# Attention products in one buffer by token blocks, with a new order of the work

## The chip, the cores and the metric

The kernel runs on one core of one Trainium2 chip. A core has five engines that work side by side, each through a queue of its own in the order in which the program issued it: TensorE (PE: matmuls, and PEld: its weight loads), VectorE (DVE), ScalarE (ACT), GpSimd (POOL) and SyncE (SP, which here only issues transfers). The metric is the time of the whole kernel on the device in microseconds. The time before is 206.82 us, the median of three runs (206.54 to 207.95).

## What is computed

The input x has 2048 tokens of 640 values. After a layer norm two branches are computed from the same normalized tokens and added to x: an attention over a sliding window, and a two-layer network.

```python
xn = layernorm(x)                                   # 2048 x 640
# A: 32 heads of 20; each token looks at 8 tokens, 2 apart, itself and back
q, k, v = split(xn @ wqkv)
logits = sum_d q[s] * k[s - 2*w], w = 0..7          # masked where s - 2*w < 0
o = sum_w softmax(logits * 20**-0.5) * v[s - 2*w]
A = o @ wo
# B: 640 -> 1536 -> 640
B = gelu(xn @ w1 + b1) @ w2 + b2
out = x + A + B
```

## The kernel before

The tokens are cut into four chunks of 512 (`NCH`, `CH`), a chunk into four blocks of 128 (`BPC`, `P`). Everything but the first normalization and the last output works on transposed data: 640 values are five tiles (`KT`) of 128 partitions, and the tokens lie along the row. The columns of the query, key and value weights are taken with a stride of 5, so that the 20 values of a head lie on 4 neighbouring partitions in all five tiles.

For each chunk:
- The rows of x are normalized (`do_xn`) and transposed: by TensorE for chunk 0 (`do_tp`, `do_tc`), by a transposing DMA of SP for the others (`do_td`, L291).
- Projections: `do_pj` (L334; for chunk 0 in smaller pieces at L347 and L378), five matmuls of 512 columns each into one of four accumulator banks, taken out to bf16 by ScalarE (`do_pc`, L398).
- Logits: VectorE multiplies the queries by the keys shifted by each window offset (`do_qk`, L431). The products lie in two buffers, `half[0]` for offsets 0 to 3 and `half[1]` for 4 to 7, each [offset, tile, 512 tokens]. The sum over the 20 values of a head is made partly by VectorE (`do_pa`, L463: tiles 0+1 and 2+3; and in chunks 2 and 3 also `do_pb`, L468: everything into tile 0) and the rest by matmuls with a 0/1 matrix (`do_lg`, L477: 24 matmuls in chunks 0 and 1, 8 in chunks 2 and 3). These write all eight offsets into one PSUM tile `L`.
- Softmax over the eight offsets (`do_cp` to `do_attn`, L513 to L554): copies, maximum, difference, exponential, sum, reciprocal by a logarithm and an exponential, product. Its small maxima and sums use `half[0]` as scratch in chunk 0.
- Expansion: a DMA of SP (`expand`, L573) writes each head's weights onto its four partitions, block by block, into `ax` for chunks 0 and 2 and into spent rows of `x_sb` for 1 and 3.
- Values: VectorE multiplies the shifted values by these weights (`do_av`, L588, one block and one half of the offsets at a time, 32 in all), adds the eight offsets up in three steps over the whole chunk (`do_add`, L597) and a last one into `oT` (`do_ot`, L602).
- The network: `do_f1` (L609) and the gelu (`do_ge`, L625) into 18 turning buffers.
- Output of chunks 0 to 2: `do_t` (L691) adds, for each fifth of the output columns, twelve products of the network in four pieces (`t..0` to `t..3`) and then five of the attention (`t..4`); ScalarE adds the bias (`do_u`, L694), SP turns it back by a transposing DMA (`do_ut`, L698), and POOL adds it by an accumulating DMA onto x in the output (`do_ud`, L703), which SP had copied there (`do_xp`, L300).
- Output of chunk 3: `do_o` (L647) with tokens on the partitions, VectorE adds x (`do_dc`, L659), and four stores follow (`do_dd`, L664). For this chunk the second bias is added to x by VectorE (`do_xl`, L304), from a copy `b2bc` of the bias in all partitions (L159).

The order of the work is written out by hand: `ORDER` (L39) names 628 pieces, and the kernel issues them one after the other; nothing is moved afterwards. A name is a function, a chunk and a part: `qk201` is `do_qk` of chunk 2, block pair 0, half 1. Each engine works through those of its own in that order, and waits where a piece needs something of another engine. GpSimd is not among the engines that are held to the order (L818).

Of the kernel before, what the change touches and what calls it, by code (L numbers as in the profile page):

```python
# [17 lines left out]
P = 128  # L18
# [15 lines left out]
LEVEL = (1, 1, 3, 3)  # L34
ACT_STATS = (2, 3)
# [4 lines left out]
pad01 pad02 st00a st00 sum1 rs00 mean1 neg1 sq1 xn00a xn00b tp00a wa tp00b wb tc00a tc00b rs01 ga xn01a xn01b gb2  # L40
tp01a gb3 tp01b tc01a tc01b gb4 gd gc0 ge st03a st02a tb hj100 st03 rs03 st02 xn03 b1 rs02 xn02 st11a st13a st10a st13
st12a st10 st12 st11 gc4 gc1 tp03 tc03 tp02 tc02 ho hj101 hc101 hj102 hc102 hj011 hc100 hc011 rs1 hj112 hc112 rc1 xn12
tc12 qk000 hj012 qk001 hj201 xn10 tc10 hc012 hc201 hj211 hc211 hj110 hc110 hj010 hc010 f10_1 pk pa000 xn13 hj111 tc13
xn11 tc11 ldx ld2 pa010 hc111 qk010 hj212 qk011 pa001 pa011 hc212 f10_5 f10_11 ge0_11 ge0_1 hj200 ge0_5 hc200 hj202
pj103 pc103 pj104 pc104 pad11 pj110 pc110 pj102 pc102 pj112 hc202 lg0 pc112 su20 cp0b cp0a m0b mask pj111 mx0b ex0b
m0a pj114 pc114 ss0b mx0a pj101 pc101 ri0b pj113 pc113 ex0a pc111 pj100 at0b pc100 ss0a su22 qk111 ri0a qk101 pj124
pc124 at0a qk110 pa111 qk100 pa110 pa101 f11_3 pa100 f11_10 ge1_3 ldo f10_8 ge0_8 hj210 hc210 xp0 su21 f10_2 ge0_2
su23 ge1_10 f10_0 ng2 ge0_0 f10_7 f10_3 f10_4 sq22 ge0_3 ge0_7 f11_5 sq21 ge0_4 sq23 f10_6 ge0_6 pj121 xs0 sq20 rs2
t040 t041 f11_0 rc2 pj122 pc122 xn22 pc121 xd0 xp1 xp2 tc22 xn23 tc23 lg1 cp1a f10_10 f11_1 ge1_1 ge1_0 xn21 av020
cp1b ge0_10 t000 t001 t042 t002 xn20 f10_9 av030 av000 f11_9 ge1_9 av001 av011 tc21 f11_11 ge0_9 tc20 ge1_5 m1 av021  # L50
mx1 ex1 av031 pj120 pc120 t003 pj123 pc123 t043 pad12 av010 pj221 pc221 ss1 pj224 ri1 ad01 at1 pc224 pj220 pj200 su33
pc220 ad00 ad02 ot0 pc200 pj214 pc214 xs1 su32 av131 pj202 pc202 pj213 pc213 pad21 pj212 pc212 su31 pj204 pj210 pc210
pc204 av121 pj211 pj203 pj201 su30 ng3 sq32 sq30 t004 u00 t044 u04 sq31 pc211 xd1 av101 av100 av111 av120 av130 sq33
ut00 t010 ud00 t011 t012 t013 t014 pc201 av110 u01 rs3 rc3 pj222 pc203 pad22 ad10 t030 t031 f11_6 xn32 tc32 t032 ad11
ad12 t020 t021 t022 xn30 tc30 f11_2 pc222 ge1_2 t023 t033 t034 xn33 tc33 t024 ge1_6 ot1 f11_4 qk201 qk200 qk210 xn31
ge1_4 qk211 pa200 pa211 pa201 u03 pa210 pb202 pb212 pb204 pj223 f12_1 pc223 f11_8 ge1_8 f12_6 ut01 ge2_6 ge2_1 pb214
t130 tc31 pj310 pc310 pj303 pc303 pj301 pc301 ge1_11 f11_7 pj311 pc311 pj302 pj312 pc302 pj313 pc312 ge1_7 pc313 u02
ut02 pj300 f13_3 f12_10 pc300 pj322 pc322 pj320 pc320 pj304 ge2_10 ut03 ut04 ud01 pad31 pc304 pj314 pc314 ud02 ge3_3
f13_9 f12_7 ge3_9 ge2_7 lg2 cp2b qk310 cp2a m2 mx2 f13_5 ge3_5 qk311 f13_2 pj324 pc324 pj321 ex2 ss2 pa311 t131 t132
t133 ri2 at2 xd2 t140 t134 ud03 pc321 u13 ge3_2 f13_7 t141 t142 t143 f13_4 f13_0 t100 ge3_7 t101 f12_11 ge2_11 pj323  # L60
t102 t103 qk300 f13_6 t104 ge3_6 f13_10 ge3_10 ge3_0 t144 u14 f12_0 ge3_4 pc323 ge2_0 qk301 xs2 pa300 pa310 pa301
pb312 pb302 pb314 f13_1 pb304 lg3 xl0 cp3a cp3b av230 ge3_1 av201 m3 av210 pad32 t110 f12_3 f12_2 t111 t112 mx3 t113
t114 u10 ut10 ex3 f12_8 f12_9 o300 av200 ss3 u11 ut11 av220 ri3 at3 av231 t120 av211 av221 o301 ud10 t121 t122 ge2_3
t123 f13_8 ge2_2 ge3_8 ge2_9 ad21 ad20 t124 xd3 xs3 ad22 u12 ut12 ot2 av321 av331 f12_5 f13_11 ge3_11 f12_4 ge2_5 t230
o310 ge2_4 av320 t231 ge2_8 t232 o320 av330 av311 av300 av310 av301 ad30 t200 ud11 t233 t201 t202 t203 o321 ud04 t204
ut13 ut14 u20 ut20 t234 ad31 u23 t210 t211 t212 t213 ud12 t214 t220 u21 t221 o322 t222 t223 t224 u22 o311 o330 o312
ud13 o313 ud20 o302 t240 ut21 t241 t242 t243 o323 t244 o331 o303 o332 o333 ad32 ot3 o324 xl1 o314 o304 dl2 ud14 dh2
dl1 u24 o334 dh1 dl0 ohi ud21 ut22 ud22 ut23 ut24 dd2 dd1 dh0 dd0 dl3 dh3 dhi dlo ud23 ud24
# [4 lines left out]
def kernel(  # L73
# [46 lines left out]
    b2bc = consts.tile([P, D], BF16, name="b2bc")  # L120
    wqkv_v = A_wqkv.rearrange("(t p) n -> p t n", p=P)
    b2_bcast = bass.AP(tensor=B_b2.tensor, offset=B_b2.offset, ap=[[0, P], [1, D]])
# [23 lines left out]
    def do_ldx():  # L146
        for n in range(2, NCH):
            load_x(n * BPC, (n + 1) * BPC)
# [7 lines left out]
    def do_ldo():  # L156
        for a, b in COLS:
            nc.sync.dma_start(wo2[:, a:b], A_wo.rearrange("(p t) n -> p t n", t=KT)[:, a:b])
        nc.sync.dma_start(b2bc[:], b2_bcast)  # L159
# [142 lines left out]
    def do_xl(pair):  # L302
        rows_ = x_sb[:, (NCH - 1) * BPC + 2 * pair : (NCH - 1) * BPC + 2 * pair + 2, :]
        nc.vector.tensor_tensor(  # L304
            out=rows_, in0=rows_, in1=b2bc[:].unsqueeze(1).to_broadcast([P, 2, D]), op=ALU.add
        )
# [106 lines left out]
    half = [prodp.tile([P, W // 2, KT, CH], BF16, name=f"half{i}") for i in range(2)]  # L413

    def window(src, h, cs):

        first = PAD - DIL * (W // 2 * h) + cs.start
        row = src[:, :, first : first + cs.stop - cs.start]
        (part, n_part), (tile_step, n_tile), (_, n_col) = row.ap
        return bass.AP(  # L420
            tensor=row.tensor,
            offset=row.offset,
            ap=[[part, n_part], [-DIL, W // 2], [tile_step, n_tile], [1, n_col]],
        )

    def do_qk(n, pair, h):
        cs = slice(pair * 2 * P, (pair + 1) * 2 * P)
        q, k, at = qkv_tile(n, 0), qkv_tile(n, 1), cs
        if n == 0:
            q, k, at = pair_of(0, pair), pair_of(1, pair), slice(0, 2 * P)  # L430
        nc.vector.tensor_tensor(  # L431
            out=half[h][:, :, :, cs],
            in0=q[:, :, at].unsqueeze(1).to_broadcast([P, W // 2, KT, 2 * P]),
            in1=window(k, h, at),
            op=ALU.mult,
        )
# [22 lines left out]
    def do_pa(n, h, c):  # L459

        cs = slice(c * 2 * P, (c + 1) * 2 * P)
        even, odd = (half[h][:, :, i : KT - 1 : 2, cs] for i in range(2))
        nc.vector.tensor_tensor(out=even, in0=even, in1=odd, op=ALU.add)  # L463

    def do_pb(n, h, t):

        first = half[h][:, :, 0, :]
        nc.vector.tensor_tensor(out=first, in0=first, in1=half[h][:, :, t, :], op=ALU.add)  # L468

    def do_lg(n):  # L470
        L = psL.tile([P, W, P], F32, tag="L", name="L")
        tiles["L", n] = L
        ts = (range(KT), (0, 2, 4), (0, 4), (0,))[LEVEL[n]]
        for h in range(2):
            for t in ts:
                for j in range(BPC):
# [3 lines left out]
                        rhs=half[h][:, :, t, j * P : (j + 1) * P],  # L480
# [13 lines left out]
    scratch = half[0][:].rearrange("p w t c -> p (w t c)")  # L494
# [4 lines left out]
    def room(n, i, dtype, off):  # L499

        size = W // 2 * P // PARTS[n] * (2 if dtype == F32 else 1)
        if PARTS[n] == 1:
            flat = attn_tile(n)[:].rearrange("p w c -> p (w c)")[:, 0:size]
        else:
            flat = scratch[:, off + i * size : off + (i + 1) * size]
# [72 lines left out]
    def do_xd(n):  # L578
        expand(nc.sync, n, (0, 1))

    def do_xs(n):
        expand(nc.sync, n, (2, 3))


    def do_av(n, j, h):
        cs = slice(j * P, (j + 1) * P)
        ws = slice(W // 2 * h, W // 2 * (h + 1))
        nc.vector.tensor_tensor(  # L588
            out=half[h][:, :, :, cs],
            in0=window(qkv_tile(n, 2), h, cs),  # L590
            in1=ax_view(n)[:, j, ws, :].unsqueeze(2).to_broadcast([P, W // 2, KT, P]),
            op=ALU.mult,
        )

    def do_add(n, k):
        a, b = ((half[0][:, 0:2], half[1][:, 0:2]), (half[0][:, 2:4], half[1][:, 2:4]), (half[0][:, 0:2], half[0][:, 2:4]))[k]
        nc.vector.tensor_tensor(out=a, in0=a, in1=b, op=ALU.add)  # L597

    def do_ot(n):
        oT = otp.tile([P, KT, CH], BF16, tag="oT", name="oT")  # L600
        tiles["oT", n] = oT
        nc.vector.tensor_tensor(out=oT[:], in0=half[0][:, 0], in1=half[0][:, 1], op=ALU.add)  # L602
# [52 lines left out]
    def do_dc(bl, hi):  # L655

        b, cs = (NCH - 1) * BPC + bl, slice(CH, D) if hi else slice(0, CH)
        room = half[1][:].rearrange("p w t c -> p (w t c)")[:, bl * D : (bl + 1) * D]
        nc.vector.tensor_tensor(out=room[:, cs], in0=out_ps(bl, hi), in1=x_sb[:, b, cs], op=ALU.add)  # L659

    def do_dd(bl, cs, eng):
        b = (NCH - 1) * BPC + bl
        room = half[1][:].rearrange("p w t c -> p (w t c)")[:, bl * D : (bl + 1) * D]
# [52 lines left out]
    for name in "tb b1 mean1 ho ldx ld2 ldo ohi mask pk".split():  # L716
# [33 lines left out]
    for n in range(NCH):  # L750
# [22 lines left out]
        for h in range(2):  # L773
            for pair in range(2):
                piece(f"qk{n}{pair}{h}", do_qk, n, pair, h)
            for j in range(BPC):
# [79 lines left out]
```

## Time and profile before

| | |
|---|---|
| median of the runs | 206.82 us |
| the profiled execution's own time | 206.68 us |
| its span, first to last instruction | 204.9 us |
| granted TensorE clock | 1.0 |
| PE / DVE / ACT / POOL busy | 98% / 91% / 62% / 10% |
| DVE, L431 and L588 (products) | 44.5 us in 16, 45.7 us in 32 |
| DVE, L463 and L468 (halvings) | 18.8 us in 16, 9.3 us in 8 |
| DVE, L597 and L602 (sums over the window) | 33.6 us in 12, 6.0 us in 4 |
| DVE, L304 (bias) | 1.6 us in 2 |
| transfers | 22.91 MB, mean 112 GB/s |

Busy is the time in which an engine has an instruction at work. Instructions overlap at their ends, so that the mean of one is longer than its pitch, the time from one start to the next in a row without waits. A row of the profile names the line, the engine, the operation, what it writes and reads, its shape (partitions x elements), how many there are, the busy time and the mean in nanoseconds, then the idle time of the engine just before them and what ended it. The span does not hold all of an execution's time: 1.8 us lie around it.

### The profile page before, as it was taken

How to read it: one execution, taken by the hardware profiler on the slowest of the kernel's cores; microseconds unless marked ns; L12 is line 12 of the kernel's file. 1: busy time of each engine (PE TensorE's matmuls, PEld its weight loads, DVE VectorE, ACT ScalarE, POOL GpSimd, SP SyncE). 2: the span in 40 equal slices, each digit the busy share in tenths (PEclk: the TensorE clock that was granted, in tenths of full speed). 3: DMA queues.
4: the chain of work that ended last, by engine and by line, in shares of the span. 5: the costliest groups of instructions: out<-in, count | busy, mean ns of one | idle time of the engine just before them, and what ended most of it. 6: DMA issues, size and time to landing. Idle time of an engine off the chain costs nothing.

```text
span 204.9 us, 2932 instructions
## 1 busy us (share of the span) xinstructions
PE 200.6 (98%) x1132; PEld 105.6 (52%) x1132; DVE 187.3 (91%) x177; ACT 128.0 (62%) x235; POOL 20.9 (10%) x33
## 2 busy tenths in 40 slices
PE   7999999999999999999999999999999999999994
PEld 2898754554444555444445554444444444445452
DVE  2899995799899999999999997999989999999963
ACT  5689967999899887858755576571785650211100
POOL 2000000000000000020010070000002207022520
PEclk9999999999999999999999999999999999999999
DMA  6997599507932027132430193044014699656635
GB/s 204 386 397 201 73 358 392 207 0 151 292 85 64 3 32 172 26 26 67 91 26 0 30 98 29 0 76 129 0 29 51 91 192 80 51 52 76 48 46 141
DMA packets 36400, 22.91 MB, mean 112 GB/s; under 512 B 24994, under 2 KB 34082, under 8 KB 36386
## 3 DMA queue, kind: packets, MB, share of 16 engines
q1 hardware_dynamic: 28144, 20.55, 36.8%
q0 software_dynamic: 7920, 1.97, 13.6%
q8 instruction: 9, 0.15, 0.3%
q10 hardware_dynamic: 322, 0.20, 0.3%
q14 instruction: 5, 0.04, 0.1%
HBM read 10.00 MB, written 4.59 MB: 71 GB/s over the span
## 4 chain that ended last, share of the span: by engine, by line
PE 96%; DMA 2%; SPq 0%; DVE 0%; issue 0%
PE T L691 27%; PE hps L609 25%; PE pps L334 24%; PE gps L378 7%; PE lo L647 5%; DMA wq_sb<-in_A_wqkv_dram 2%; PE both L647 2%; PE L L477 2%; PE gps L347 1%; PE hi L647 1%; PE tp L279 0%; SPq L126 0%; DVE half L659 0%; PE tb L454 0%
## 5 line engine op out<-in xcount | busy, mean ns | idle before, releaser
L609 PE MATMUL hps<-xnT,w_sb 128*128 128x512 bf16 x240 | 55.9, 379 | 0.0
L431 DVE TENSOR_TENSOR half<-qT,kT 128x5120 bf16<-128x5120 bf16 x16 | 44.5, 2821 | 1.4 <-PE L L477 1.4
L691 PE MATMUL T<-hT,w_sb 128*128 128x512 bf16 x180 | 42.8, 379 | 0.0
L609 PEld LDWEIGHTS <-w_sb 128*128 128x128 bf16 x240 | 23.3, 98 | 27.9 <-issue 0.8
L703 POOL DMA_DIRECT2D out_dram<-x_sb x15 | 19.5, 1406 | 176.8 <-DMA x_sb<-x_sb 176.7
L691 PEld LDWEIGHTS <-w_sb 128*128 128x128 bf16 x180 | 17.3, 98 | 20.6 <-issue 0.4
L625 ACT ACTIVATE hT<-hps,bT 128x512 bf16<-128x512 f32 x36 | 23.7, 693 | 6.2 <-PE hps L609 6.1
L694 ACT ACTIVATE x_sb<-T,bT 128x512 bf16<-128x512 f32 x15 | 10.3, 689 | 23.4 <-PE T L691 23.4
L588 DVE TENSOR_TENSOR half<-vT,ax 128x2560 bf16<-128x2560 bf16 x16 | 23.1, 1485 | 1.4 <-PE L L477 1.4
L588 DVE TENSOR_TENSOR half<-vT,x_sb 128x2560 bf16<-128x2560 bf16 x16 | 22.6, 1486 | 0.0
L597 DVE TENSOR_TENSOR half<-half,half 128x5120 bf16<-128x5120 bf16 x8 | 22.3, 2821 | 0.1
L463 DVE TENSOR_TENSOR half<-half 128x2048 bf16<-128x2048 bf16 x16 | 18.8, 1221 | 0.0
L691 PE MATMUL T<-oT,wo 128*128 128x512 bf16 x75 | 18.1, 379 | 0.0
L334 PE MATMUL pps<-xnT,wq_sb 128*128 128x512 bf16 x75 | 18.1, 379 | 0.0
L334 PE MATMUL pps<-xnT,wk_sb 128*128 128x512 bf16 x75 | 18.0, 379 | 0.0
L334 PE MATMUL pps<-xnT,wv_sb 128*128 128x512 bf16 x75 | 18.0, 379 | 0.0
L172 ACT ACT_TABLE_LOAD x12 | 15.4, 1283 | 0.9 <-PEq L840 0.7
L334 PEld LDWEIGHTS <-wv_sb 128*128 128x128 bf16 x75 | 8.8, 117 | 7.6
L334 PEld LDWEIGHTS <-wk_sb 128*128 128x128 bf16 x75 | 8.7, 118 | 7.6 <-issue 0.4
L262 ACT ACTIVATE xn<-x_sb,nmr,rstd 128x640 bf16<-128x640 bf16 x12 | 10.8, 921 | 2.9 <-DVE nmr L252 2.2
L334 PEld LDWEIGHTS <-wq_sb 128*128 128x128 bf16 x75 | 8.8, 117 | 7.2
L398 ACT CAST vT<-pps 128x512 bf16<-128x512 f32 x15 | 8.6, 580 | 5.8 <-PE pps L334 5.8
(95 smaller groups left out, 232.1 us busy)
## 6 DMA issues: line engine op xcount, KB each, us to landing
ax<-attn SPq DMA_DIRECT2D x8, 256.0 KB, 4.3
x_sb<-attn SPq DMA_DIRECT2D x8, 256.0 KB, 4.7
x_sb<-in_A_x_dram SPq DMA_DIRECT2D x3, 640.0 KB, 6.2
w_sb<-in_B_w_dram SPq DMA_DIRECT2D x2, 960.0 KB, 11.3
w_sb<-in_B_w_dram SPq DMA_DIRECT2D x4, 480.0 KB, 8.7
out_dram<-x_sb SPq DMA_DIRECT2D x3, 640.0 KB, 7.3
out_dram<-x_sb POOLq DMA_DIRECT2D x15, 128.0 KB, 4.0
wq_sb<-in_A_wqkv_dram SPq DMA_DIRECT2D x1, 800.0 KB, 5.1
```

The source lines that it names most:

```text
L172: nc.scalar.preload_act_table_set(name)
L334: nc.tensor.matmul(ps[:], lhsT=wqkv_p[which][:, ti, to, :], rhs=xnT[:, ti, :], start=(ti == 0), stop=(ti == KT - 1),)
L378: nc.tensor.matmul(ps[:, to - a, :], lhsT=wqkv_p[which][:, ti, to, :], rhs=tiles["xnT", 0][:, ti, pair * 2 * P : (pair + 1) * 2 * P], star ...
L431: nc.vector.tensor_tensor(out=half[h][:, :, :, cs], in0=q[:, :, at].unsqueeze(1).to_broadcast([P, W // 2, KT, 2 * P]), in1=window(k, h, at ...
L463: nc.vector.tensor_tensor(out=even, in0=even, in1=odd, op=ALU.add)
L588: nc.vector.tensor_tensor(out=half[h][:, :, :, cs], in0=window(qkv_tile(n, 2), h, cs), in1=ax_view(n)[:, j, ws, :].unsqueeze(2).to_broadca ...
L597: nc.vector.tensor_tensor(out=a, in0=a, in1=b, op=ALU.add)
L609: nc.tensor.matmul(ps[:], lhsT=w1_sb[:, ti, ft * P : (ft + 1) * P], rhs=tiles["xnT", n][:, ti, :], start=(ti == 0), stop=(ti == KT - 1),)
L625: nc.scalar.activation(hT, tiles["hps", n, ft][:], ACT.Gelu_apprx_tanh, bias=bT[:, ft : ft + 1], scale=1.0)
L647: nc.tensor.matmul(out_ps(bl, hi), lhsT=lhs, rhs=rhs[:, CH:D] if hi else rhs[:, 0:CH], start=pc == 0 and k == 0, stop=pc == 4 and k == len ...
L691: nc.tensor.matmul(ps[:], lhsT=lhs, rhs=rhs, start=pc == 0 and k == 0, stop=pc == 4 and k == len(srcs) - 1)
L703: nc.gpsimd.dma_start(dst, src, accum_op=ALU.add)
```

## The change

- One buffer `prod` [block, offset, tile, 128 tokens] replaces the two halves, so that all products of a block of 128 tokens lie together. `do_qk` and `do_av` make the products of one block with all eight offsets in one instruction: 16 of 128x5120 each.
- `do_pa` adds tiles 2 and 3 onto tiles 0 and 1 (not odd onto even) for a pair of blocks and all offsets: 8 of 128x4096. `do_pb` adds tile 1, then tile 4, for the chunk: 4 of 128x4096. The logits matmuls are as many as before and read the new places.
- The sum over the window becomes `do_ac` (a block, 128x2560, 16), `do_ad` (a pair of blocks, 128x2560, 8) and `do_ot` (a pair of blocks, 128x1280, 8).
- The second bias of the last chunk is added to x by one accumulating DMA of POOL (`do_xb`) that reads the bias from HBM once for each token; `b2bc`, its load and the two additions of VectorE go.
- The expansions become pieces of one block (`xe`), chunk 0's softmax scratch moves to `ax`, and the x of chunk 2 is loaded in two transfers.
- GpSimd is held to the order too, and `ORDER` is new throughout. The table `BY_DMA` could move sums to POOL; it is empty.

```diff
-    half = [prodp.tile([P, W // 2, KT, CH], BF16, name=f"half{i}") for i in range(2)]
+    prod = prodp.tile([P, BPC, W, KT, P], BF16, name="prod")
-    def do_qk(n, pair, h):
+    def do_qk(n, j):
         nc.vector.tensor_tensor(
-            out=half[h][:, :, :, cs],
-            in0=q[:, :, at].unsqueeze(1).to_broadcast([P, W // 2, KT, 2 * P]),
-            in1=window(k, h, at),
+            out=prod[:, j],
+            in0=q[:, :, at].unsqueeze(1).to_broadcast([P, W, KT, P]),
+            in1=window(k, at),
...
+    def rows_of(a, b):
+        return prod[:, a:b].rearrange("p j w t c -> p (j w) (t c)")
+    def do_pa(pair):
+        rows = rows_of(2 * pair, 2 * pair + 2)
+        low, high = rows[:, :, 0 : 2 * P], rows[:, :, 2 * P : 4 * P]
+        nc.vector.tensor_tensor(out=low, in0=low, in1=high, op=ALU.add)
+    def do_pb(t):
+        rows = rows_of(0, BPC)
+        first = rows[:, :, 0:P]
+        nc.vector.tensor_tensor(out=first, in0=first, in1=rows[:, :, t * P : (t + 1) * P], op=ALU.add)
...
-                        rhs=half[h][:, :, t, j * P : (j + 1) * P],
+                        rhs=prod[:, j, W // 2 * h : W // 2 * (h + 1), t, :],
...
-    def do_av(n, j, h):
+    def do_av(n, j):
-            out=half[h][:, :, :, cs],
+            out=prod[:, j],
...
+    def do_ac(n, j):
+        low, high = (prod[:, j, W // 2 * h : W // 2 * (h + 1)] for h in range(2))
...
+            nc.vector.tensor_tensor(out=low, in0=low, in1=high, op=ALU.add)
+    def do_ad(n, pair):
+        low, high = (prod[:, 2 * pair : 2 * pair + 2, 2 * i : 2 * i + 2].rearrange("p j w t c -> p j (w t c)") for i in range(2))
+        nc.vector.tensor_tensor(out=low, in0=low, in1=high, op=ALU.add)
+    def do_ot(n, pair):
+        oT = get(("oT", n), lambda: otp.tile([P, KT, CH], BF16, tag="oT", name="oT"))
+        a, b = (prod[:, 2 * pair : 2 * pair + 2, w].rearrange("p j t c -> p t j c") for w in range(2))
+        out = oT[:, :, 2 * pair * P : (2 * pair + 2) * P].rearrange("p t (j c) -> p t j c", j=2)
+        nc.vector.tensor_tensor(out=out, in0=a, in1=b, op=ALU.add)
...
-    def do_xl(pair):
-        rows_ = x_sb[:, (NCH - 1) * BPC + 2 * pair : (NCH - 1) * BPC + 2 * pair + 2, :]
-        nc.vector.tensor_tensor(
-            out=rows_, in0=rows_, in1=b2bc[:].unsqueeze(1).to_broadcast([P, 2, D]), op=ALU.add
-        )
+    def do_xb():
+        rows_ = x_sb[:, (NCH - 1) * BPC :, :]
+        b2_all = bass.AP(tensor=B_b2.tensor, offset=B_b2.offset, ap=[[0, P], [0, BPC], [1, D]])
+        nc.gpsimd.dma_start(rows_, b2_all, accum_op=ALU.add)
...
-        for n in range(2, NCH):
-            load_x(n * BPC, (n + 1) * BPC)
+        for n in (4, 5, 6):
+            load_x(n * BPC // 2, (n + 1 + n // 6) * BPC // 2)
...
-    engines = {getattr(mybir.EngineType, e) for e in ("PE", "DVE", "Activation", "SP")}
+    engines = {getattr(mybir.EngineType, e) for e in ("PE", "DVE", "Activation", "SP", "Pool")}
```

Of the order, the places that the prediction speaks of (old, then new):

```
- tp00a wa tp00b wb ... ga xn01a xn01b gb2 tp01a gb3 tp01b tc01a
+ wa ... tp00a ... tp00b ... ga xn01a wb gb2 tp01a xn01b st03a tc01a
- tc12 ... tc10 ... tc13 ... tc11 ldx ld2
+ tc11 ... tc10 ... ldx ... tc13 tc12 ... ld2
- xs0 ... xd0 xp1 xp2 ... tc22 ... tc23 ... tc21 ... tc20
+ tc22 ... tc20 ... xe02 ... xe03 tc23 xe00 ... tc21 ... xe01 ... pj210
- ... ad32 ot3 o324 xl1 o314 o304 ... o334 ... ohi
+ ... ot30 ... o304 ... o314 ... ot31 dl1 ... o324 ... o334 ... ohi
```

More of the change, by code (lines that the diff above doesn't have):

```diff
@@ L34 @@
 LEVEL = (1, 1, 3, 3)
+BY_DMA = ((), (), (), ())
 ACT_STATS = (2, 3)
@@ L45 @@
[L45 to L49, printed above, removed]
@@ L805 @@
         last = BPC - 1
-        for pair in range(2):
-            piece(f"xl{pair}", do_xl, pair)
         for bl in range(BPC):
```

132 lines of the change are left out of this document (58 added, 74 removed).

## The prediction

> **What bounds the kernel now.** I read the page first (busy shares, slices, chain), then the groups by shape, the waits, and the timeline of each engine. The page says that TensorE is the bound from almost the first microsecond to the last:
>
> ```profile
> span 204.9 us, 2932 instructions
> PE 200.6 (98%) x1132; PEld 105.6 (52%) x1132; DVE 187.3 (91%) x177; ACT 128.0 (62%) x235; POOL 20.9 (10%) x33
> PE   7999999999999999999999999999999999999994
> PEclk9999999999999999999999999999999999999999
> PE 96%; DMA 2%; SPq 0%; DVE 0%; issue 0%
> ```
>
> A busy PE need not be PE at its peak, so I checked the pitch: in the chain "1.08 PE hps x5" repeats, that is 0.216 us for each 512-column matmul at a granted clock of 1.0, and from 6.32 us (the first real product, released by the load of wq) to 202.17 us (the last one) piece follows piece with no gap over 0.3 us. Around these 195.85 us lie 6.3 us of head and 2.7 us of tail. The span is 204.9 and the execution's own time 206.68, so 1.78 us lie outside the span; 206.68 is 0.14 below the median of the runs (206.82).
>
> Now VectorE, which the change is about. By shape:
>
> ```profile
> L431 DVE TENSOR_TENSOR half<-qT,kT 128x5120 bf16<-128x5120 bf16 x16 | 44.5, 2821 | 1.4 <-PE L L477 1.4
> L588 DVE TENSOR_TENSOR half<-vT,ax 128x2560 bf16<-128x2560 bf16 x16 | 23.1, 1485 | 1.4 <-PE L L477 1.4
> L597 DVE TENSOR_TENSOR half<-half,half 128x5120 bf16<-128x5120 bf16 x8 | 22.3, 2821 | 0.1
> L463 DVE TENSOR_TENSOR half<-half 128x2048 bf16<-128x2048 bf16 x16 | 18.8, 1221 | 0.0
> ```
>
> And who is late for whom:
>
> ```profile
> DVE half L588 <- PE L L477: 1.4, 2, 0.9
> DVE half L431 <- PE L L477: 1.4, 1, 1.4
> PEld L477 <- DVE x_sb L304: 0.4, 1, 0.4
> PEld L477 <- DVE half L463: 0.4, 1, 0.4
> ```
>
> VectorE waits for TensorE (it cannot overwrite the products until the logits matmuls L477 have read them). The other way round only two weight loads wait, 0.4 us each, and the matmul row shows no gap there. So the two engines run abreast, VectorE just ahead. The change can win on TensorE only what lies in the head and the tail, and can lose as soon as VectorE, or a transfer, comes late.
>
> **VectorE, part by part.** In the timeline four L431 take 11.03 us and eight L588 take 11.30, so one starts (11.03 - 2.82)/3 = 2.74 us and (11.30 - 1.49)/7 = 1.40 us after the one before. Between the two sizes that is 0.522 ns an element and 0.067 us fixed; it gives 1.135 us for 2048 elements, and the four L463 (4.63 us) give 1.14. By this an instruction of 4096 elements costs 2.20 and one of 1280 costs 0.735. Then:
> - Query-key products: 16 of 5120 before and after; no change.
> - Attention-value products: 32 x 1.40 become 16 x 2.74: -1.1.
> - First halvings: 16 x 1.14 become 8 x 2.20: -0.6. Second ones: 8 x 1.14 become 4 x 2.20: -0.3.
> - Sums over the window: 12 x 2.74 + 4 x 1.40 = 38.5 become 16 x 1.40 (one block each) + 8 x 1.40 (pairs) + 8 x 0.735 = 39.5: +1.1.
> - The two bias additions (L304): 2 x 0.735 go: -1.5.
>
> Sum: -2.3 us of 187.3. The new products have rows of 128 columns where L431 had 256. Nearest row with 128 columns: L588, 2 x 1.40 = 2.80 for 5120 elements, so at most 16 x 0.06 = 1.0 us come back; the other end, 0, is the one I take because the L588 rows lie on the same line as L463 with its 256-column rows.
>
> **What takes the place of the halves.** Before, the products of window offsets 0 to 3 and 4 to 7 lay in two buffers, and the first half was free when its 12 (or 4) logits matmuls were done: the first L588 starts at 56.71 us, before the 24 matmuls from 55.83 are through at 57.3. One buffer by blocks is read by both halves, so VectorE must now wait for all: 0.7 us lost once behind chunk 1's logits, 0.25 behind the 8-matmul ones. This is part of what the 2.3 us pay for.
>
> **Is VectorE still in time?** I put the new order on the measured pieces: matmul groups at 0.216 us for 512 columns (five: 1.08) and 0.055 for 128, logits 1.41 and 0.55, ScalarE at its pitches (eviction 0.48, gelu and bias eviction 0.58, normalization 0.83, table load 1.29), and added up each queue in its order, starting a piece when its inputs are there. The same sum over the old order puts the four logits at 31.7, 56.0, 123.7 and 148.7 us; the trace has them at 31.4, 55.8, 123.6 and 148.7. The new order, with TensorE never pausing, gives: logits of chunk 0 at 32.8 (VectorE is through 0.8 us before), chunk 1 at 58.4 (0.3 before), chunk 2 at 126.3 (0.7), chunk 3 at 151.3 (0.7). The output projections ask for oT at 85.1 us (chunk 0, ready 0.5 before), 131 (26 before), 177.7 (1.2), and in the last chunk at 194.6 for blocks 0 and 1 (0.4) and 198.6 for blocks 2 and 3 (0.5). All margins are positive, about as thin as the two 0.4 us rows above. Behind the last logits VectorE has 8 x 2.74 + 8 x 1.40 + 4 x 1.40 + 4 x 0.735 + 3.6 (softmax) + 0.3 = 45.6 us; the old tail had 45.7 by the same count and took 46.1 (149.10 to 195.23), so I add 0.5 for dependent neighbours and 0.2 for the first expansion: 151.8 + 46.3 = 198.1 against 198.6. The last pieces of TensorE after that (two blocks and the last 128 columns, 3.4 us), and the four stores, are those of before: the tail stays at 2.7.
>
> **The head.** The two warming matmuls that stood in the gap before wq landed are moved into the busy stretch: 2 x 0.055 = +0.11. VectorE now does a statistics half (L208, 0.47) before the copy of the second block's transposed columns, which ended at 7.79 while its reader, by the pitch, ran at 8.03; it moves to about 8.1 or 8.2: +0.1 (ends 0 and 0.47).
>
> **The queues.** SP issues as many transfers as before (one x load more, the bias rows' load less). The x loads move ahead of two of chunk 1's transposes, and the 256 KB expansions of chunk 0 mix with the transposes of chunk 2, whose last is issued at 58.9 and would land near 62.3 (1.2 to 1.4 us for each transfer ahead of it) for a projection due at 62.6. So 0 here, with margins of 0.4 and 0.3. ScalarE loads 14 tables instead of 12: 2 x 1.29 us, in the sums above, beside 77 idle microseconds. POOL: the accumulating DMA stands fifth, waits for ScalarE's last read of the last chunk's x (87 us), and is issued near 110 us behind four others. The 15 like it took 1.41 us each on POOL and landed in 3.8 to 6.1 us; this one has the same 512 rows of five times the size. Ends: 4 and 5 x 6.1 = 30 us, at most to 140; its first reader is at 197 and the next on POOL is due at 152. So 0, covered by 57 us at least. The 160 KB load of the bias rows goes (-1.7 us of SP near 31 us, which nobody waited for).
>
> **Sum.** 206.68 + 0.11 + 0.1 - 0 = **206.9 us**; I take nothing off for VectorE's 2.3 us, because no TensorE gap in the trace is theirs.
>
> **Rivals.**
> (A) Slower: the x loads get between chunk 1 and its transposes. Before:
>
> ```profile
> 16.75 6.95 SPq L291 DMA_TRANSPOSE xnT<-xn  x4
> 23.76 1.12 SPq L126 DMA_DIRECT2D x_sb<-in_A_x_dram  x2
> DMA to landing us min/median/max: 2.4/2.4/4.0
> x_sb<-in_A_x_dram SPq DMA_DIRECT2D x3, 640.0 KB, 6.2
> ```
>
> All four transposes were issued before the x loads. Now 1.31 MB start at 19.4 to 21.1 us, and the last two transposes are issued at 22.9 and 24.1. At the 390 GB/s of the page's best slices the loads need 3.4 us, to about 24.4; then two transposes of 1.2 us: the last lands near 27.0, and chunk 1's first projection is due at 27.4. If the loads take the 6.2 to 8.1 us to land that their rows show, and the transposes start only then, that projection starts at 29.1 to 31.0: 1.7 to 3.6 us lost, 208.6 to 210.5. It decides from a landing 0.4 us later than I reckon. For it: a transpose near other traffic took 4.0. Against: those 6.2 us were themselves behind two transposes and ahead of the w2 loads.
> The Trainium skill (DMA: Bandwidth & Descriptors, Queues, rings and completion order) says that each DMA engine takes the descriptors of a ring in order, so a transpose cannot pass the copies ahead of it. The 4.0 beside 2.4 us agrees with that but does not prove it.
> (B) VectorE, or a transpose behind the expansions, is 0.5 to 1.5 us late at one thin margin (58.4 us, 62.6 us for chunk 2's first projection, or the tail, where an expansion that lands in the 5.7 us of one row instead of 4.5 costs 1.2 - 0.5 = 0.7): 207.4 to 208.4.
> (C) Faster: the 2.3 us reach the end, 204.5. That needs a TensorE gap that VectorE sets; the rows show none, and head and tail are set by a load and by stores.
> (D) The products by blocks do nothing at all to the end, and the head loses nothing either: 206.7, inside the forecast.
>
> **Chances.** Forecast with D 0.62, B 0.20, A 0.15, C 0.03. 1% (about 2.1 us) is about what a measurement of this kernel can tell from no change. Faster by more: C, 0.03. Slower by more: most of A and the top of B, 0.16. Within: 0.81. Range 206.3 to 208.9: the low end is the head unchanged with a few tenths of scatter, the high end B and the start of A.
>
> **What would show it.** Right: TensorE busy for 195.9 to 196.3 us without a gap from 6.3 us on, VectorE near 185 us busy, longer waits of VectorE for the logits. A would show as a TensorE gap at 27 us before the first pps piece, released by a transpose; B as one at a logits group, at 62 us, or before the last oT products; C as a shorter chain with less TensorE in it. Wrong altogether would be a 5120-element instruction over 2.9 us or a matmul pitch over 0.216.

## The result, and the profile after

The changed kernel takes 209.05 us (median of 6 runs, 208.58 to 209.33) against 206.78 for the kernel before on the same chip (6 runs): a ratio of 1.0101, 95% interval 1.0078 to 1.0124. That is 2.2 us slower than the 206.9 of the prediction, at the edge of "within 1%", and in plain microseconds 0.15 above the end of its range (208.9). The profiled execution took 208.97 us with a span of 206.6. Some executions of a kernel come in a slower state (one of e3 took 212.87 us at a granted clock of 0.984, against 207.52 at 1.0), and the medians below are those of the other executions.

The page of the changed kernel, against the lines of before: busy shares, the slices of TensorE and its granted clock, the chain.

```profile
span 206.6 us, 2900 instructions
PE 200.6 (97%) x1114; PEld 106.0 (51%) x1132; DVE 184.8 (89%) x163; ACT 130.2 (63%) x237; POOL 22.3 (11%) x34
PE   8999989999999999999999999999999999999994
PEclk9999999999999999999999999999999999999999
PE 81%; ACT 13%; DMA 2%; issue 2%; DVE 0%
```

TensorE is still the bound and its clock is untouched, but its row now has an 8 at the sixth slice (26 to 31 us), and the chain of the work that ended last leaves TensorE for ScalarE and a DMA for 15% of the span, where before it was TensorE for 96%. VectorE has 2.5 us less to do, as the sum had it (2.3). By groups:

```profile
L428 DVE TENSOR_TENSOR prod<-qT,kT 128x5120 bf16<-128x5120 bf16 x16 | 44.4, 2820 | 2.4 <-ACT qT L395 1.8
L582 DVE TENSOR_TENSOR prod<-vT,ax 128x5120 bf16<-128x5120 bf16 x8 | 22.2, 2820 | 2.7 <-PE L L478 2.7
L463 DVE TENSOR_TENSOR prod<-prod 128x4096 bf16<-128x4096 bf16 x8 | 18.0, 2285 | 0.0
L595 DVE TENSOR_TENSOR prod<-prod 128x2560 bf16<-128x2560 bf16 x16 | 23.3, 1484 | 0.1
```

A product of 128x5120 in rows of 128 columns costs 2.82 us as it did in rows of 256, so the 0 of the prediction was the right end. The waits of the changed kernel (what waited, for whom: total, times, longest):

```profile
DVE prod L582 <- PE L L478: 2.7, 2, 1.8
PEld L331 <- DMA xnT<-xn: 1.2, 1, 1.2
PE pps L331 <- ACT trash L218: 0.7, 1, 0.7
PEld L478 <- DVE prod L469: 0.4, 1, 0.4
PE pps L331 <- DMA xnT<-xn: 0.4, 1, 0.4
```

New are the three lines of L331, the projections. Two of them are matmuls that came late; the timeline of TensorE shows where:

```profile
24.76 2.32 PE L612 MATMUL hps<-xnT,w_sb 128*128 128x512 bf16 x10
27.77 1.25 PE L331 MATMUL pps<-xnT,wk_sb 128*128 128x512 bf16 x5 [0.69 <-ACT trash L218]
...
62.58 0.81 PE L694 MATMUL T<-hT,w_sb 128*128 128x512 bf16 x2
63.78 1.24 PE L331 MATMUL pps<-xnT,wk_sb 128*128 128x512 bf16 x5 [0.39 <-DMA xnT<-xn]
```

At a pitch of 0.216 us the ten matmuls from 24.76 are through at 26.92; the first projection of chunk 1 starts at 27.77, 0.85 us later. From 62.58 a group of three runs (one of its records is missing), three pitches to 63.23, and the first projection of chunk 2 starts at 63.78, 0.55 us later. The first pause is put down to ScalarE (its statistics, L218), but ScalarE was through with that line at 27.23, 0.54 us before the projection starts, and the weight load of the same piece waits 1.2 us for a transpose; which of the two it was is the matter of e1. The queue of SP shows what stands ahead of both:

```profile
16.51 2.62 SPq L289 DMA_TRANSPOSE xnT<-xn  x2
19.18 1.60 SPq L125 DMA_DIRECT2D x_sb<-in_A_x_dram  x3
22.58 2.53 SPq L289 DMA_TRANSPOSE xnT<-xn  x2
...
54.37 1.30 SPq L575 DMA_DIRECT2D ax<-attn  x2
55.76 2.99 SPq L289 DMA_TRANSPOSE xnT<-xn  x1
58.81 0.59 SPq L575 DMA_DIRECT2D ax<-attn  x1
59.49 2.38 SPq L289 DMA_TRANSPOSE xnT<-xn  x1
```

The two transposes issued from 22.58 on stand behind three x loads, the last one of chunk 2 (59.49) behind an expansion issued 0.7 us earlier. By the DMA view of each stretch they land 4.5, 3.8 and 4.3 us after their issue; behind nothing, in both kernels, it is 2.4.

With the two executions side by side, all of the difference has a place:

| stretch | before | after | difference |
|---|---|---|---|
| start of the span to the first product | 6.32 | 6.22 | -0.10 |
| first product to the end of the last matmul | 195.84 | 197.29 | +1.45 (pauses 0.85 + 0.55) |
| end of the last matmul to the end of the span | 2.74 | 3.09 | +0.35 |
| outside the span | 1.78 | 2.37 | +0.59 |
| sum | 206.68 | 208.97 | +2.29 |

Three theories follow. (1) The pauses are transposes that land late behind copies on SP's queue; rival: ScalarE's statistics, which the profile names. (2) What lies outside the span is longer because of the accumulating DMA; rival: because of something else in the changed kernel. (3) VectorE's saving is worth nothing because TensorE is the bound; rival: it is worth something, and is hidden under the losses.

### The profile page after: what moved, and what is told of

Read it like the earlier page. It is cut to its first block, busy times and chain, and to the rows that moved or that the text cites. A ratio compares the mean times of both kernels' runs of the same rounds, so it can differ in the third digit from the quotient of the medians.

```text
span 206.6 us, 2900 instructions
## 1 busy us (share of the span) xinstructions
PE 200.6 (97%) x1114; PEld 106.0 (51%) x1132; DVE 184.8 (89%) x163; ACT 130.2 (63%) x237; POOL 22.3 (11%) x34
## 4 chain that ended last, share of the span: by engine, by line
PE 81%; ACT 13%; DMA 2%; issue 2%; DVE 0%
PE T L694 25%; PE pps L331 20%; PE hps L612 17%; PE lo L650 5%; PE gps L375 5%; ACT hT L628 3%; PE idle L441 2%; PE both L650 2%; DMA xnT<-xn 2%; ACT xn L260 2%; ACT L170 2%; ACT trash L218 2%; PE hi L650 2%; PE gps L344 1%; PE L L478 1%
## 5 line engine op out<-in xcount | busy, mean ns | idle before, releaser
L428 DVE TENSOR_TENSOR prod<-qT,kT 128x5120 bf16<-128x5120 bf16 x16 | 44.4, 2820 | 2.4 <-ACT qT L395 1.8
L694 PE MATMUL T<-hT,w_sb 128*128 128x512 bf16 x175 | 44.1, 379 | 0.4 <-issue 0.2
L628 ACT ACTIVATE hT<-hps,bT 128x512 bf16<-128x512 f32 x36 | 24.1, 685 | 7.8 <-PE hps L612 7.2
L582 DVE TENSOR_TENSOR prod<-vT,ax 128x5120 bf16<-128x5120 bf16 x8 | 22.2, 2820 | 2.7 <-PE L L478 2.7
L595 DVE TENSOR_TENSOR prod<-prod 128x2560 bf16<-128x2560 bf16 x16 | 23.3, 1484 | 0.1
L582 DVE TENSOR_TENSOR prod<-vT,x_sb 128x5120 bf16<-128x5120 bf16 x8 | 22.3, 2819 | 0.1
L331 PE MATMUL pps<-xnT,wk_sb 128*128 128x512 bf16 x72 | 18.0, 379 | 1.2 <-ACT trash L218 0.7
L331 PE MATMUL pps<-xnT,wv_sb 128*128 128x512 bf16 x74 | 18.1, 379 | 0.1
L463 DVE TENSOR_TENSOR prod<-prod 128x4096 bf16<-128x4096 bf16 x8 | 18.0, 2285 | 0.0
L331 PE MATMUL pps<-xnT,wq_sb 128*128 128x512 bf16 x74 | 17.9, 379 | 0.0
L331 PEld LDWEIGHTS <-wk_sb 128*128 128x128 bf16 x75 | 8.6, 118 | 9.2 <-DMA xnT<-xn 1.2
L395 ACT CAST kT<-pps 128x512 bf16<-128x512 f32 x15 | 8.6, 586 | 7.5 <-PE pps L331 7.4
L331 PEld LDWEIGHTS <-wq_sb 128*128 128x128 bf16 x75 | 8.8, 117 | 7.5
L331 PEld LDWEIGHTS <-wv_sb 128*128 128x128 bf16 x75 | 8.7, 118 | 7.2
```

Of the source, the lines that this page charges most:

```text
L331: nc.tensor.matmul(ps[:], lhsT=wqkv_p[which][:, ti, to, :], rhs=xnT[:, ti, :], start=(ti == 0), stop=(ti == KT - 1),)
L395: nc.scalar.copy(dest[:, to, off : off + CH], tiles["pps", n, which, to][:])
L428: nc.vector.tensor_tensor(out=prod[:, j], in0=q[:, :, at].unsqueeze(1).to_broadcast([P, W, KT, P]), in1=window(k, at), op=ALU.mult,)
L463: nc.vector.tensor_tensor(out=low, in0=low, in1=high, op=ALU.add)
L582: nc.vector.tensor_tensor(out=prod[:, j], in0=window(qkv_tile(n, 2), slice(j * P, (j + 1) * P)), in1=ax_view(n)[:, j, :, :].unsqueeze(2).t ...
L595: nc.vector.tensor_tensor(out=low, in0=low, in1=high, op=ALU.add)
```

## The experiments

Twelve kernels, each beside the kernel before on the same chip. "Outside" is the difference of time and span, median over the runs.

**e1: one x load goes behind the transposes.** The 640 KB of the last chunk's x become a piece of their own, issued after chunk 1's last transpose.

```diff
-        for n in (4, 5, 6):
-            load_x(n * BPC // 2, (n + 1 + n // 6) * BPC // 2)
+        for n in (4, 5):
+            load_x(n * BPC // 2, (n + 1) * BPC // 2)
+    def do_ldy():
+        load_x(3 * BPC, 4 * BPC)
-... ldx ... tc13 tc12 ...
+... ldx ... tc13 tc12 ldy ...
```

> The changed kernel, with the 640 KB load of the last chunk's x issued behind chunk 1's two late transposes instead of ahead of them; the two 320 KB loads stay ahead. Theory 1 (the transposes queue behind the x loads): 0.66 MB less lies ahead, 1.7 us at 390 GB/s, so the last transpose lands 3.8 - 1.3 = 2.5 us after its issue instead of 3.8, the TensorE pause before the first chunk-1 projection (27.77 us, 0.85 us long) goes, and the time falls by 0.6 to 0.9 us, to about 208.3. Rival (ScalarE, which the waits name for 0.7 us there, gives the accumulator bank back too late): the transpose lands earlier but the pause stays at 0.3 us or more and the time falls by less than 0.5.

Measured: 208.02 us, ratio 1.005 (1.0034 to 1.0067), 1.0 less than the changed kernel. In the timeline of TensorE the first pause is gone (below it, the end of ScalarE's statistics):

```profile
24.67 2.32 PE L615 MATMUL hps<-xnT,w_sb 128*128 128x512 bf16 x10
26.82 1.24 PE L334 MATMUL pps<-xnT,wk_sb 128*128 128x512 bf16 x5
...
62.74 1.24 PE L334 MATMUL pps<-xnT,wk_sb 128*128 128x512 bf16 x5 [0.30 <-DMA xnT<-xn]
```

```profile
26.94 0.20 ACT L221 ACTIVATION_READ_ACCUMULATOR trash<-x_sb 128x1 f32 x1
```

The projection starts 2.15 us after the row ahead of it, ten pitches, and the transposes land 2.4 us after their issue. ScalarE does the same work and is through with those statistics at 27.14, after the projection has started at 26.82. So the projection had no need of them, and the name "ACT trash" in the wait was wrong: the cause is the transpose. The second pause stays.

**e2: one expansion goes behind chunk 2's last transpose.**

```diff
-... t001 xe00 su31 pa11 ... lg1 av03 tc21 ge0_6 ...
+... t001 su31 pa11 ... lg1 av03 tc21 xe00 ge0_6 ...
```

> The changed kernel, with one expansion of chunk 0 (block 0) issued behind the last transpose of chunk 2 instead of ahead of it. Theory 1 (same cause, second place): that transpose lands near 62 us instead of 63.7, the 0.55 us pause of TensorE at 63.2 us goes, VectorE does not miss the block because it takes it third (66.0 us): 0.4 to 0.6 us less, 208.5. Rival (the pause comes from ScalarE's late normalization, which ended at 59.0): the pause stays, and the time is that of the changed kernel, 209.0.

Measured: 208.76 us, ratio 1.010 (1.0067 to 1.0134). The timeline of TensorE:

```profile
27.70 1.25 PE L331 MATMUL pps<-xnT,wk_sb 128*128 128x512 bf16 x5 [0.64 <-ACT trash L218]
...
62.50 0.81 PE L694 MATMUL T<-hT,w_sb 128*128 128x512 bf16 x2
63.15 1.24 PE L331 MATMUL pps<-xnT,wk_sb 128*128 128x512 bf16 x5
```

The second pause is gone and the first stays. The span is 205.9 in the profile, 0.7 less, but 206.35 in the median of six runs, only 0.25 less. The times alone would not have shown it: 0.3 us against an interval of plus or minus 0.7.

**e3: both moves.**

> Both moves of the two runs before. Theory 1: both pauses go, TensorE is busy without a pause again and its last matmul ends near 202.2 us instead of 203.5; time 1.2 to 1.4 us less, 207.7; what is then left over the old kernel (0.9 us) lies in the stores and outside the span. Rival (VectorE's new products or other thin margins cost the rest): a pause opens elsewhere and less than 0.8 us are won.

Measured: 207.52 us, ratio 1.0033 (1.0014 to 1.0053); no pause over 0.2 us is left in the row of TensorE, the last matmul ends at 202.22 (before: 202.16), and the span is 205.1 in the profile. Theory 1 holds: the two moves take back 1.5 of the 2.3 us. What is left over the kernel before (206.82 beside these runs) is 0.7, and of that 0.64 lies outside the span (2.41 against 1.77).

**e4: no accumulating DMA.** The changed kernel without `xb`; the last chunk's output lacks the second bias.

> The changed kernel without the accumulating DMA, so that the second bias is left out of the last chunk. Theory 2 (the 0.6 us that the changed kernel takes outside its span, 2.4 against 1.8, belong to this DMA): the time less the span falls back to 1.8 and the time by 0.6, to 208.4, with the same span. Rival (they come from elsewhere, such as GpSimd's queue being held to the order, or from the slower stores at the end): time and span stay at 209.0 and 206.6.

Measured: 208.49 us, ratio 1.0082 (1.0054 to 1.011), 0.56 less than the changed kernel, at the same span (206.6 in the profile, where the matmuls end 0.33 us later and the tail is as much shorter). Outside lie 1.99 us (1.84 to 2.07 over the runs) instead of 2.40: 0.4 of the 0.6 that theory 2 had expected to go.

**e5: the kernel before with its x loads ahead of two of chunk 1's transposes**, nothing else.

```diff
-... pk pa000 xn13 hj111 tc13 xn11 tc11 ldx ld2 ...
+... pk pa000 ldx xn13 hj111 tc13 xn11 tc11 ld2 ...
```

> The kernel before, with one thing of the change done to it: the x loads of the last two chunks (2 x 640 KB) are issued ahead of two of chunk 1's four transposes (order on SP: two transposes, the x loads, two transposes). Nothing else differs. Theory 1 (the transposes stand behind the copies): the last of those transposes lands 3.8 us or more after its issue instead of 2.4, near 27 us, TensorE pauses by 1 to 2 us ahead of the first projection of chunk 1 (25.9 us in the trace of before), and the time is 207.6 to 208.8. Rival (the pause of the changed kernel came from its other order of work on ScalarE and TensorE, which this kernel does not have): no pause, 206.8.

Measured: 209.23 us, ratio 1.0124 (1.0111 to 1.0137): 2.5 us slower, more than expected. The waits, and the row of TensorE with the pause:

```profile
PEld L334 <- DMA xnT<-xn: 2.7, 1, 2.7
PE pps L334 <- DMA xnT<-xn: 2.4, 1, 2.4
```

```profile
24.27 1.80 PE L378 MATMUL gps<-xnT,wv_sb 128*128 128x256 bf16 x15
28.47 2.35 PE L334 MATMUL pps<-xnT,wq_sb 128*128 128x512 bf16 x10 [2.40 <-DMA xnT<-xn]
```

Here no instruction of ScalarE is named, and the kernel before has none of the changed kernel's order on its engines: one move of SP's queue is enough. The same place in the kernel before:

```profile
24.28 1.80 PE L378 MATMUL gps<-xnT,wv_sb 128*128 128x256 bf16 x15
25.92 2.32 PE L334 MATMUL pps<-xnT,wq_sb 128*128 128x512 bf16 x10
```

So the reader of the transposes is due 1.64 us behind the start of the row ahead, at 25.91 in e5, where it was due at 26.92 in the changed kernel. The transposes land 6.7 and 5.9 us after their issue, the last at 28.4, where it was 27.7 in the changed kernel. The same 1.31 MB ahead of them cost 2.56 us here and 0.85 there: 1.0 of the difference is that the changed order had put chunk 1's first projection later, 0.7 that the transposes landed earlier.

**e7: the kernel before without VectorE's two bias additions**; its last chunk lacks the second bias.

> The kernel before without VectorE's two bias additions, so that the last chunk's output lacks the second bias; VectorE has 1.5 us less to do in the stretch that ends the kernel, and no accumulating DMA takes their place. Theory (TensorE is the bound, what VectorE saves does not reach the end): 206.8, within 0.3, with VectorE's busy time down from 187.3 to 185.8. Rival (VectorE's time reaches the end, the case C of the prediction): 205.3.

Measured: 206.62 us, ratio 0.9998 (0.9983 to 1.0014), with VectorE at this:

```profile
PE 200.5 (98%) x1132; PEld 105.7 (52%) x1132; DVE 185.7 (91%) x175; ACT 127.7 (62%) x235; POOL 20.9 (10%) x33
```

1.6 us of VectorE's work taken out of the last stretch change nothing. VectorE only waits longer: 1.23 us for the logits of chunk 3, where it waited 0.50. The rival of theory 3 falls for that stretch. Both additions stood ahead of waits for TensorE, so of VectorE's other stretches e7 says nothing; there the evidence is TensorE's row without gaps.

**e9: the kernel before with the bias by the accumulating DMA.**

```diff
-        nc.sync.dma_start(b2bc[:], b2_bcast)
...
-    def do_xl(pair):
-        rows_ = x_sb[:, (NCH - 1) * BPC + 2 * pair : (NCH - 1) * BPC + 2 * pair + 2, :]
...
+    def do_xb():
+        rows_ = x_sb[:, (NCH - 1) * BPC :, :]
...
+        nc.gpsimd.dma_start(rows_, b2_all, accum_op=ALU.add)
```

> The kernel before with only its bias for the last chunk changed: one accumulating DMA on POOL instead of two additions by VectorE and the load of the bias rows. Theory 2 (the accumulating DMA lengthens what lies outside the span, and nothing within it): span as before, 204.7 to 205.2, outside the span 2.4 us instead of 1.8, time 207.2 to 207.5. Rival (it is hidden, as the prediction costed it, and the 0.55 us are a matter of the changed kernel's other parts): 206.8, outside the span 1.8.

Measured: 206.74 us, ratio 1.0011 (0.9996 to 1.0025), outside 1.77. Theory 2 falls as I had put it: in the kernel before the same DMA costs nothing. The scheduler had put it second on POOL (100.31 us), while the changed kernel has it fifth; so place and size were tried next.

**e12: the same DMA fifth on POOL, behind four stores**, by holding POOL to the written order as well. In the expectations of e12 and e11 "theory 3" means that the place decides, and not (3) above.

```diff
-    engines = {getattr(mybir.EngineType, e) for e in ("PE", "DVE", "Activation", "SP")}
+    engines = {getattr(mybir.EngineType, e) for e in ("PE", "DVE", "Activation", "SP", "Pool")}
```

> The kernel before with the bias of its last chunk by the accumulating DMA as in e9, but fifth on POOL, behind four stores, as the changed kernel has it (the order of POOL is written out for this). Theory 3 (the place decides): outside the span 2.4, time 207.3. Rival (the cost belongs to the changed kernel's end, where POOL's last stores are issued 2 to 3 us later): 206.8, outside the span 1.8.

Measured: 206.69 us, ratio 1.0 (0.9992 to 1.0009), outside 1.76. The place is not it.

**e8: the changed kernel with that DMA for one block of 128 tokens**; the other three blocks of the last chunk lack the second bias.

```diff
-        rows_ = x_sb[:, (NCH - 1) * BPC :, :]
+        rows_ = x_sb[:, (NCH - 1) * BPC : (NCH - 1) * BPC + 1, :]
```

> The changed kernel with the accumulating bias DMA for one block of 128 tokens instead of four (160 KB, 128 rows of descriptors; the other three blocks of the last chunk lack the second bias). The DMA stays fifth on POOL. If its size sets what it costs outside the span: 1.8 to 2.0 us there, 208.5 to 208.6 as without it (e4). If that it is there at all does: 2.4, 209.05.

Measured: 209.11 us, ratio 1.0128 (1.0107 to 1.015), outside 2.42. A quarter of the bytes, landed in 5.3 us instead of 10.2, cost as much outside the span. The size is not it either.

**e11: e3 with the DMA second on POOL.**

```diff
-... ud00 ... ud03 xb ud10 ...
+... ud00 xb ... ud03 ud10 ...
```

> The changed kernel with both moves of SP's transfers (as in e3: last chunk's x load and one expansion behind the transposes) and the accumulating bias DMA second on POOL instead of fifth, as it stood in e9, where it cost nothing. Theory 3 (what the bias DMA costs outside the span depends on its place among POOL's stores): outside the span 1.8 us instead of 2.4, time 207.0. Rival (it costs that in this kernel wherever it stands): outside the span 2.4, time 207.6 as e3.

Measured: 215.34 us, ratio 1.0424 (1.0404 to 1.0444), far from both; outside 2.41. The edit did more than I meant. In the written order the DMA now precedes the normalization of one of the last chunk's blocks, which therefore reads x with the bias added, and has to wait for the DMA to land: issued at 91.25, it takes 10.6 us, and ScalarE, idle for 6.6 us, starts at 101.89; that block's transpose and the projections behind it wait in turn. The row of TensorE, and two lines of the page, busy and granted clock by slices of 5.3 us:

```profile
99.03 1.24 PE L697 MATMUL T<-oT,wo 128*128 128x512 bf16 x5
105.37 2.30 PE L334 MATMUL pps<-xnT,wk_sb 128*128 128x512 bf16 x5 [5.11 <-DMA xnT<-xn]
107.47 2.34 PE L334 MATMUL pps<-xnT,wq_sb 128*128 128x512 bf16 x5
109.60 1.46 PE L615 MATMUL hps<-xnT,w_sb 128*128 128x512 bf16 x5
```

```profile
PE   7999999999999999998199999999999999999994
PEclk9999999999999999999769999999999999999999
```

A pause of 5.1 us, and then matmuls at twice their pitch for some 4 us. For the question it was meant for it gives one thing: outside lie 2.41 us with the DMA in the second place too.

**e13: e3 with one more VectorE instruction of 1280 elements near chunk 1's logits.**

```diff
+    def do_sp():
+        nc.vector.tensor_tensor(out=spare[:], in0=spare[:], in1=spare[:], op=ALU.add)
-... pa10 ... su31 pa11 ge0_7 ... lg1 ...
+... pa10 ... su31 pa11 sp ge0_7 ... lg1 ...
```

> The changed kernel with both moves (e3) and one more VectorE instruction of 1280 elements (0.81 us by the bias addition in e10, on a tile that nothing reads) ahead of chunk 1's second halvings. In e3 VectorE is through 0.26 us before the logits of chunk 1 start (58.01 against 58.27). Theory (margins as thin as the prediction's sums gave them, 0.3 here): a pause of TensorE of 0.5 to 0.6 ahead of those logits, which nothing gives back: 208.1. Rival (VectorE has slack, its waits of 1.8 us behind those logits take it up): no pause, 207.6.

Measured: 207.34 us, ratio 1.004 (1.0025 to 1.0054), no pause. It does not test the margin: as the diff shows I put the instruction behind the last halving (`pa11`) and not ahead of the halvings, so the logits did not have to wait for it. VectorE's timeline shows what it did meet:

```profile
53.54 4.49 DVE L466 TENSOR_TENSOR prod<-prod 128x4096 bf16<-128x4096 bf16 x2
57.94 0.82 DVE L478 TENSOR_TENSOR spare<-spare 128x1280 bf16<-128x1280 bf16 x1
59.81 5.56 DVE L591 TENSOR_TENSOR prod<-vT,ax 128x5120 bf16<-128x5120 bf16 x2 [1.05 <-PE L L487]
```

The wait for the logits shrinks from 1.8 to 1.05 us and the next product starts when it did (59.80 in e3). So the wait that the single buffer brings has room for 0.8 us of other work. What a late halving would do was not tried.

**e10: e3 with the bias by VectorE again, and the warming matmul back in the head's gap.** The two additions stand in VectorE's waits for the logits of chunks 2 and 3.

```diff
-... pb24 pj304 ... pb34 lg3 ... xb ...
+... pb24 xl0 pj304 ... pb34 xl1 lg3 ...
-... tc00b rs01 ga xn01a wb gb2 ...
+... wb tc00b rs01 ga xn01a gb2 ...
```

> The changed kernel with its three costs undone: the load of the last chunk's x and one expansion issued behind the transposes that they stood ahead of, the bias of the last chunk by VectorE again (two additions, put where VectorE waits for the logits of the last two chunks), and the warming matmul back in the gap of the head. If the account of pauses, DMA outside the span and head is complete: span 204.8 to 205.2, outside the span 1.8, time 206.7 to 207.0, equal to the kernel before. If the products by blocks have a cost of their own on TensorE's path: 207.3 or more. If they are worth something: below 206.5.

Measured: 207.53 us, ratio 1.0043 (1.0027 to 1.006). The additions cost TensorE nothing, outside lie 1.74 us again, and the last matmul ends at 202.15 (before: 202.16). So the time lies where a cost of the products on TensorE's path was to put it (207.3 or more), but that path is as long as before. What is longer is the span: 205.8 in the median, 0.7 more than in e3, and in the profile 205.6 against 205.1. The stores do not make that difference, for the last one (32 KB) lands at 204.23 in both traces. It lies behind that landing, in the order of the waits with which SP ends the program. By the SP view, e10 and then e3:

```profile
SPq L859 <- DMA out_dram<-x_sb: 0.6, 1, 0.6
SPq L859 <- DMA out_dram<-prod: 1.3, 1, 1.3
```

```profile
SPq L853 <- DMA out_dram<-x_sb: 0.9, 1, 0.9
SPq L853 <- DMA out_dram<-prod: 0.3, 1, 0.3
```

In e10 SP waits for that last store right behind POOL's, and seven more waits follow at 0.06 us each, for what is done by then; in e3 it stands last. From the last landing to the end of the span it is 1.32 us in e10, 0.89 in e3 and 0.90 in the kernel before. Against the kernel before, the profiled execution of e10 takes 0.65 us longer (207.33 and 206.68): 0.42 are these waits, and 0.24 the landing of the last store (1.72 us instead of 1.48). So e10 misses its 206.7 to 207.0 by 0.5, and no version of the changed kernel that I ran beats the kernel before.

### What lies outside the span stays open

| kernel | VectorE instructions | POOL instructions | bias DMA | outside, us |
|---|---|---|---|---|
| before; e5; e7 | 177; 177; 175 | 33 | none | 1.77; 1.84; 1.80 |
| e9, e12 | 175 | 34 | second, fifth | 1.77, 1.76 |
| after, e1, e2, e3 | 163 | 34 | fifth | 2.40, 2.42, 2.41, 2.41 |
| e11, e8 | 163 | 34 | second; fifth, one block | 2.41, 2.42 |
| e13 | 164 | 35 | fifth | 2.18 |
| e4 | 163 | 33 | none | 1.99 |
| e10 | 165 | 33 | none | 1.74 |

Shown is that the 0.6 us belong to the changed kernel and not to the DMA as such; that taking the DMA out of the changed kernel saves 0.4 of them (0.56 in time); that neither its size nor its place matters; and that two added instructions that move no data of use (e13) take 0.2 off as well. That last row speaks against any account by transfers. Something in how the programs of the engines end is a guess that no run here separates.

## Why the prediction was wrong by 2.2 us, and where it was right

- **TensorE is the bound, nothing off for VectorE's saving: right.** First product to last matmul is 197.29 us, less 1.40 of pauses 195.89, against 195.84 before. e7 shows the same from the other side: 1.6 us of VectorE gone, ratio 0.9998. Case C had no ground.
- **VectorE's sum: right.** 2.5 us less for 2.3 predicted; 4096 elements took 2.285 in the mean for a pitch of 2.20, rows of 128 columns cost nothing extra. (Its items as written add up to 2.4, and from 38.5 to 39.5 it is +1.0 and not +1.1, which makes 2.5.)
- **VectorE in time, by the queue sums: right, at times thinner.** In e3, where TensorE does not pause, the logits start at 32.54, 58.27, 126.26 and 151.30 us (told: 32.8, 58.4, 126.3, 151.3), and VectorE is through 0.25 us before those of chunk 1 (0.3), 0.5 before chunk 2's (0.7) and 0.24 before chunk 3's (0.7). No logits group and no last oT product was late; that half of case B did not come. The longer waits of VectorE behind the logits came, a little longer than told: 0.91 us became 1.79 at chunk 1 (0.7 more told) and 0.50 became 0.91 at chunk 3 (0.25 more told).
- **The head, +0.21: wrong, but small.** The first product started 0.10 us earlier, and of the 1.45 us up to the last matmul only 0.05 are not pauses.
- **The queues, "So 0 here, with margins of 0.4 and 0.3": this step failed.** It reckoned the last transpose of chunk 1 to land at 27.0 for a reader due at 27.4; it landed at 27.7 (3.85 us behind its issue at 23.84) for a reader that stood ready at 26.92. For chunk 2 it reckoned 62.3 for 62.6; the transpose landed at 63.7 (4.25 us behind its issue at 59.49) for a reader ready at 63.23. So the landings came 0.7 and 1.4 us later than reckoned (0.6 of the 1.4 is a later issue, 59.49 for 58.9), and the first reader 0.5 earlier. Two margins of a few tenths were entered as zeros, although the sums for both could be off by more; they cost 0.85 and 0.55 (1.0 and 0.5 by the times of e1 and e3).
- **Case A: its place and mechanism were right, its price was too high here** (1.7 to 3.6 told, 0.85 to 1.0 came), and right for the kernel before, where the same move costs 2.5 (e5). The transposes-late half of case B came as well, so two of the rivals that were held to be alternatives happened together. That 209.05 lies within A's 208.6 to 210.5 is luck: A's own price here would have made 207.8, and the second pause, the tail and the time outside the span brought the rest. The Trainium skill (DMA: Bandwidth & Descriptors, Queues, rings and completion order) has each DMA engine take the descriptors of one ring in order, though a later one may finish its write first. The runs agree with the order: the same transpose lands 3.8 to 4.5 us after its issue behind x loads and 2.4 when the last of them is issued behind it (e1). None of the transposes looked at here landed ahead of a copy issued before it.
- **The accumulating DMA, "So 0": right for its transfer, wrong for the total.** It landed in 10.2 us, 77 us ahead of its first reader, and in the kernel before it costs nothing (e9, e12). But in the changed kernel 0.4 us outside the span go with it (e4; 0.56 by the times), and another 0.2 there without it. The sum had taken over the 1.78 us outside the span unchanged; why they grew stays open.
- **The tail, "stays at 2.7": 0.35 short.** The last store, of 32 KB, landed in 1.8 us instead of 1.5. By the DMA views behind 195.5 us, before and then after:

```profile
out_dram<-half ACTq DMA_DIRECT2D x1, 32.0 KB, 1.5
out_dram<-prod ACTq DMA_DIRECT2D x1, 32.0 KB, 1.8
```

The last store of POOL is issued at 200.12 instead of 197.00 and lands at 204.33, when the 32 KB store, issued at 203.87, is under way. The traces of the fourteen kernels fit that. The 32 KB store took 1.48 or 1.49 us where POOL's had landed before its issue (before, e5, e7, e9, e12) and 1.64 to 1.92 where POOL's had 0.36 us or more to go (after, e1, e2, e3, e8, e10, e11, e13); in e4, with 0.13 us to go, it took 1.48. No run moves POOL's store alone, so the cause is argued, not shown.

## What to carry to other kernels

When TensorE has no gap, a change elsewhere can win only in the head and the tail, and can lose anywhere: look at each margin that it leaves, and enter a transfer that lands a few tenths ahead of its reader as a likely cost and not as zero. In these runs a transpose issued behind copies on the same queue landed after them, so bulk loads that nobody waits for go behind it. And a wait that names a compute engine which has long been done should be read as a DMA until a run says otherwise; in e8 the same pause bears the name of yet another line of ScalarE (L628).

## What the runs showed of the hardware that was not expected

- A pause of 5.1 us halved TensorE's clock: in e11 the granted clock fell to 0.50 at 103.2 us, 2.9 us behind the last matmul's end, and was back at 1.0 at 110.0, 4.7 us after the matmuls had started again. The last matmul ended 7.4 us later than in e3, so 2.3 us came on top of the pause. The pause of 2.4 us in e5 left the clock at 1.0. The Trainium skill (TensorE: Matmul & The Clock Gate, Part 1: The HAM clock gate) has the clock fall to half after an idle window of about 3.4 us. Both pauses fit that, but the moment of the fall does not: behind the last matmul of these fourteen traces it came after 2.4 us (e13) to 4.9 us (e10). So a pause of 2.4 us is not shown to be safe.
- The same two transposes behind the same 1.31 MB of x landed in 4.5 and 3.8 us in the changed kernel and in 6.7 and 5.9 in e5. Most of that is that e5 issues them 1.4 us sooner; by the time of the trace they landed at 27.1 and 27.7, and at 27.8 and 28.4. Those 0.7 us are still more than the margins of 0.4 and 0.3 that the prediction took them against.
- The order of the waits that end the program counts: in e10 seven of them stand behind the last landing, 0.43 us in all.
- Time outside the span is not a constant of the kernel: it went from 1.74 to 2.42 us over these kernels, and repeats within 0.25 us from run to run of each.
